# Attention and mixture of experts on one core: full 128-wide tiles for the narrow transposes, and another order in the last batch

## The chip, the core and the metric

The kernel runs on one core of one Trainium2 chip. The metric is device time in microseconds (us). The engines are TensorE (PE in the profile; its weight loads are PEld), VectorE (DVE), ScalarE (ACT), GpSimd (POOL) and SyncE (SP), which here issues most DMAs.

## The reference

For 8 batches (B), 8 heads, 576 tokens (S) and 64 columns a head, keys and values are averaged over 8 neighbouring tokens, so that each head has 72 pooled keys, and attention runs over those. The result, 4608 tokens of 512 columns, goes through a mixture of 4 groups of 4 experts, each expert 512 to 1024 to 512; a token goes to the best expert of its best group.

```python
k_p = k.reshape(B, H, Sp, pool, D).mean(axis=3)          # v_p the same; pool = 8, Sp = 72
scores = scale * np.matmul(q, k_p.transpose(0, 1, 3, 2))
attn = np.exp(scores - scores.max(-1)); attn = attn / (attn.sum(-1) + 1e-09)
x = np.matmul(attn, v_p)                                  # (B*S, H*D), heads side by side
...
g_idx = argmax(x @ w_group); g_w = softmax(x @ w_group)[g_idx]
e_idx = argmax(x @ w_expert[g_idx]); e_w = softmax(...)[e_idx]
out = g_w * e_w * (relu(x @ w1[g, e]) @ w2[g, e])         # float32 in and out
```

## The kernel before

**Tiling.** A batch's 576 queries are cut into five chunks (`CH`), four of 128 and chunk 4 of 64. The four pairs of heads are `g` = 0 to 3; a pair has 144 pooled keys: 128 in a main tile and 16 that are left, the "remainder". All products that must be exact in float32 are made of two parts, a rounded high one and the low rest (`fp32r`): ScalarE copies the high part out of PSUM, VectorE subtracts it to make the low one.

**A chunk's attention** goes through these steps, each a method: `qb` (VectorE transposes the queries, line 283), `sc` (TensorE scores, 289), `mx` and `sb` (VectorE maximum and subtraction, 296 and 302, ScalarE exponential, 303), `su_` (VectorE sum and reciprocal, 308 to 310), `nm` (GpSimd divides: two remainder products at 318, the main one at 322), `px_` (TensorE transposes the remainder's probabilities, 329; ScalarE copies, 330), `pxd` (VectorE low part, 334), `pm` and `pmd` (the same for the main ones: 341, 343, 347). Then `av` (356) multiplies with the values, `rt` (369) makes the router's logits in 40 rows, `route` (377) transposes them to tokens on partitions. Before a batch's chunks, `kb` and `kt` scale and transpose its keys: four full tiles (261) and the remainder's zero-padded ones, `krz` (266).

**The experts.** In each batch one expert, the one that most tokens want, is applied densely to the whole batch: `up` (525; ScalarE relu 527, VectorE low part `upd` 532) in eight blocks of two halves, 256 and 320 tokens, 12 products each; `down` (546, for the 64-token chunk 556; ScalarE scales and writes, 551 and 552) in 14 steps. `split` makes high and low parts of the weights: ScalarE at 510, GpSimd (or VectorE, where the plan says `:v`) at 511. Tokens that wanted another expert (`Left`) are gathered, multiplied and scattered in blocks of 32; here one block holds them, and it runs inside the last batch: `step` (placement), `which` (the block's batch and expert, converted to integers at 661), `fetch_x`, `fetch_a`, `fetch_b` (loads on SP), `whole` and `turn` (add the two parts, transpose, 725 and 735), `gather` (743), `up`, `down` (757, 773; scatter by an indirect DMA on GpSimd).

**Order.** Plans written by hand as strings set the order: START, FIRST (batch 0), STEADY (batches 1 to 6) and LAST (batch 7). In a plan `m.` is the batch whose experts run, `n.` the attention of the next batch, `x.` the one after it, `l.` the leftover. So during batch 3's `up`, TensorE also does the scores and transposes of batch 4. TensorE, SP and VectorE keep the plan's order everywhere; ScalarE and GpSimd do so in START only and are ordered by a scheduler elsewhere. PSUM has three buffers for `mm`, one for `sc`, three for `tp`.

Of the kernel before, what the change touches and what calls it, by code (L numbers as in the profile page):

```python
# [8 lines left out]
F32 = mybir.dt.float32  # L9
# [4 lines left out]
ALU = mybir.AluOpType  # L14
# [71 lines left out]
def attn_moe(ctx: ExitStack, tc: tile.TileContext, q, k, v, wg, we, w1, w2, out):  # L86
# [35 lines left out]

    wr = keep.tile([128, 4, 20], F32, name="wr")
# [24 lines left out]
    krz = wk.tile([32, 2, 2, D], F32, name="krz")  # L148
# [10 lines left out]
    class Att:  # L159


        def __init__(s, b):
            s.b = b
            s.xt = s.lt = s.vp = s.kp = s.rp = s.q = s.rem = None
            s.k, s.v, s.qT, s.p, s.px, s.ss, s.su, s.tp, s.ta, s.m = {}, {}, {}, {}, {}, {}, {}, {}, {}, {}

# [91 lines left out]
        def kt(s):  # L258
# [21 lines left out]
        def qb(s, c):  # L280
            o, n = CH[c]
# [3 lines left out]
        def sc(s, c):  # L285
            n = CH[c][1]
# [5 lines left out]
        def mx(s, c):  # L292
            n = CH[c][1]
# [4 lines left out]
        def sb(s, c):  # L298
            n = CH[c][1]
# [5 lines left out]
        def su_(s, c):  # L305
            n = CH[c][1]
# [5 lines left out]
        def nm(s, c, eng="p"):  # L312
            n = CH[c][1]
            p, su = s.p[c], s.su[c]
            eng = nc.vector if eng == "v" else nc.gpsimd
            px = s.px[c] = sm.tile([128, 2, 3, 2, 16], F32, name="px")
            for z in range(2):
                eng.tensor_tensor(  # L318
                    out=px[0:n, z], op=ALU.mult,
                    in0=p[0:n, z].rearrange("p (y x) s -> p y x s", x=2)[:, :, 1, 56:72].unsqueeze(1).broadcast_to([n, 3, 2, 16]),  # L320
                    in1=su[0:n, z].rearrange("p (y x) -> p y x", x=2)[:, :, 1:2].unsqueeze(1).broadcast_to([n, 3, 2, 16]))
# [547 lines left out]
```

## Time and profile before

| | |
|---|---|
| median of 3 runs | 608.69 us (605.95 to 609.57) |
| profiled execution | 606.4 us, of which the span is 604.6 |
| granted TensorE clock, mean | 0.992 |
| busy: TensorE, VectorE, ScalarE, GpSimd | 587.3 (97%), 391.8 (65%), 279.5 (46%), 258.7 (43%) |
| DMA | 81.31 MB, mean 134 GB/s |

The span runs from the first instruction to the last; the execution's time includes what lies around it. Busy shares are means over the whole span, so they say little of a stage. In rows of the trace a name such as `tp<-ident,px 128*96` is what is written and read, with the shape that is loaded into TensorE; L329 is line 329 of the kernel above. A float32 product, such as a score, counts as two instructions in the trace (a group of four stands as x8), a transpose as one.

### The profile page before, as it was taken

The page shows a single profiled execution, that of the slowest core. Times are in us where ns is not written, and L with a number is a line of the kernel's source. Part 1 is how long each engine was busy: PE and PEld are TensorE (multiplying, and loading weights), DVE is VectorE, ACT ScalarE, POOL GpSimd, SP SyncE. Part 2 cuts the span into 40 slices and gives each one's busy share as a digit, 9 for nine tenths or more (in the row PEclk, how much of TensorE's full clock was granted, in tenths as well). Part 3 has the DMA queues.
Part 4 walks back from the last instruction along what each step waited for, and adds up shares of the span by engine and source line. Part 5 has one row for each costly group of instructions (what it writes and reads, how often), then busy time and mean ns, then how long its engine had stood idle before and what let it go on. Part 6 is the DMA issues. An engine that isn't in the chain of part 4 may idle for free.

```text
span 604.6 us, 10902 instructions
## 1 busy us (share of the span) xinstructions
PE 587.3 (97%) x3863; PEld 527.3 (87%) x3863; DVE 391.8 (65%) x996; ACT 279.5 (46%) x581; POOL 258.7 (43%) x268
## 2 busy tenths in 40 slices
PE   8889999999999999999999999999999999999995
PEld 8888888899978998899978998899978998899874
DVE  4468998599662877459672876459672884347321
ACT  2476554365446445364445445364535543253121
POOL 3366443076416552375406553366225552343100
PEclk9799999999999999999999999999999999999999
DMA  7759135555435460663425561783516200641911
GB/s 195 205 160 212 39 70 131 182 175 125 98 105 191 151 115 37 227 214 53 100 88 195 166 114 35 257 303 83 110 63 220 78 1 2 207 151 52 383 47 41
DMA packets 119209, 81.31 MB, mean 134 GB/s; under 512 B 76774, under 2 KB 95718, under 8 KB 118768
## 3 DMA queue, kind: packets, MB, share of 16 engines
q1 hardware_dynamic: 110464, 70.80, 40.0%
q10 hardware_dynamic: 8656, 9.74, 4.9%
q8 instruction: 32, 0.52, 0.4%
q14 instruction: 25, 0.20, 0.1%
q0 software_dynamic: 32, 0.04, 0.0%
HBM read 75.01 MB, written 28.38 MB: 171 GB/s over the span
## 4 chain that ended last, share of the span: by engine, by line
PE 79%; DVE 10%; DMA 4%; ACT 2%; SPq 2%; issue 1%; POOL 0%; ACTq 0%; POOLq 0%; DVEq 0%
PE mm L525 28%; PE mm L546 26%; PE tp L356 6%; PE sc L289 6%; PE mm L556 5%; DVE kp L208 3%; PE tp L341 2%; SPq L203 2%; DMA wr<-in_moe_w_expert_dram 1%; DVE ht L532 1%; PE tp L329 1%; DMA kv<-in_k_dram 1%; DMA q<-in_q_dram 1%; DMA sw<-in_moe_w_dram 1%; ACT kb L233 1%
## 5 line engine op out<-in xcount | busy, mean ns | idle before, releaser
L525 PE MATMUL mm<-xt,w 128*128 128x256 f32 (+1 forms) x1536 | 222.7, 300 | 1.3 <-DVE ht L532 1.3
L525 PEld LDWEIGHTS mm<-xt,w 128*128 128x128 f32 x1536 | 207.6, 189 | 3.7 <-DVE ht L532 1.5
L546 PE MATMUL mm<-w,ht 128*128 128x512 f32 x768 | 187.8, 396 | 0.0
L546 PEld LDWEIGHTS mm<-w,ht 128*128 128x128 f32 x768 | 140.8, 188 | 29.4 <-issue 0.8
L511 POOL TENSOR_TENSOR w<-sw,w 128x1024 fp32r<-128x1024 f32 x52 | 128.0, 2482 | 81.1 <-ACT w L510 75.6
L527 ACT ACTIVATE ht<-mm 128x256 fp32r<-128x256 f32 (+1 forms) x128 | 52.4, 409 | 112.0 <-PE mm L525 111.2
L532 DVE SCALAR_TENSOR_TENSOR ht<-mm,ht 128x256 fp32r<-128x256 f32 (+1 forms) x192 | 60.4, 345 | 35.6 <-ACT ht L527 35.3
L510 ACT CAST w<-sw 128x1024 fp32r<-128x1024 f32 x64 | 65.7, 1047 | 19.0 <-PE mm L525 9.9
L318 POOL TENSOR_TENSOR px<-p,su 128x96 f32<-128x96 f32 (+1 forms) x80 | 26.7, 355 | 110.6 <-DVE su L310 53.1
L296 DVE TENSOR_REDUCE mx<-sc 128x8 f32<-128x576 f32 (+1 forms) x40 | 30.0, 750 | 37.8 <-PE sc L289 37.8
L289 PE MATMUL sc<-kT,qT 128*128 128x144 f32 (+1 forms) x320 | 48.4, 296 | 1.6 <-DVE dg L387 0.6
L322 POOL TENSOR_TENSOR p<-p,su 128x576 f32<-128x576 f32 (+1 forms) x40 | 46.0, 1149 | 3.1
L289 PEld LDWEIGHTS sc<-kT,qT 128*128 128x128 f32 (+1 forms) x320 | 43.3, 186 | 3.9 <-issue 1.2
L551 ACT ACTIVATE y<-mm,gm 128x512 f32<-128x512 f32 x32 | 21.9, 685 | 34.4 <-PE mm L546 34.3
L361 DVE TENSOR_TENSOR xt<-tp,xt 128x320 fp32r<-128x320 f32 (+2 forms) x68 | 29.5, 439 | 11.5 <-ACT xt L357 9.7
L211 POOL TENSOR_TENSOR kv<-kv 128x512 f32<-128x512 f32 x14 | 18.1, 1292 | 43.8 <-DMA kv<-in_v_dram 35.6
L303 ACT ACTIVATE p<-p 128x576 f32<-128x576 f32 (+1 forms) x40 | 27.3, 683 | 20.2 <-DVE p L302 20.0
L562 DVE TENSOR_TENSOR y<-mm,y 64x512 f32<-64x512 f32 x8 | 5.4, 681 | 44.9 <-ACT y L561 44.9
L308 DVE TENSOR_REDUCE su<-p 128x8 f32<-128x576 f32 (+1 forms) x40 | 29.8, 746 | 5.5 <-ACT p L303 4.5
L357 ACT CAST xt<-tp 128x320 fp32r<-128x320 f32 (+2 forms) x68 | 26.1, 385 | 15.7 <-PE tp L356 13.9
L302 DVE TENSOR_TENSOR p<-sc,mx 128x576 f32<-128x576 f32 (+1 forms) x40 | 30.2, 755 | 3.7
L556 PE MATMUL mm<-w,ht 128*128 128x512 f32 x128 | 30.5, 389 | 0.0
(214 smaller groups left out, 724.5 us busy)
## 6 DMA issues: line engine op xcount, KB each, us to landing
sw<-in_moe_w_dram SPq DMA_DIRECT2D x72, 512.0 KB, 4.1
xscr<-xt SPq DMA_DIRECT2D x8, 2304.0 KB
kv<-in_v_dram SPq DMA_DIRECT2D x16, 512.0 KB
out_dram<-y ACTq DMA_DIRECT2D x32, 256.0 KB, 2.0
q<-in_q_dram SPq DMA_DIRECT2D x112, 72.0 KB, 2.5
kv<-in_k_dram SPq DMA_DIRECT2D x14, 512.0 KB, 5.4
kv<-in_moe_w_dram SPq DMA_DIRECT2D x6, 512.0 KB
ph<-xscr SPq DMA_DIRECT2D x2, 1152.0 KB
```

The costliest lines, as they stand in the source:

```text
L289: nc.tensor.matmul(ps[0:n, g // 2, 144 * (g % 2):144 * (g % 2) + 144], lhsT=s.qT[c][:, g, 0:n], rhs=s.kT[:, g, :], start=(g % 2 == 0), sto ...
L296: red(out=mx[0:n], in_=scv, axis=AX.X, op=ALU.max)
L302: tt(out=p[0:n], in0=scv, in1=mx[0:n].unsqueeze(3).broadcast_to([n, 2, 4, SP]), op=ALU.subtract)
L322: eng.tensor_tensor(out=p[0:n], in0=p[0:n], in1=su[0:n].unsqueeze(3).broadcast_to([n, 2, 4, SP]), op=ALU.mult)
L356: nc.tensor.matmul(ps[:, 0:n], lhsT=flat(l[:, g]), rhs=r, start=(i == 0), stop=(i == len(ops) - 1))
L510: nc.scalar.copy(out=wh, in_=raw)
L511: (nc.vector if eng == "v" else nc.gpsimd).tensor_tensor(out=wl, in0=raw, in1=wh.bitcast(F32), op=ALU.subtract)
L525: nc.tensor.matmul(ps[:, 0:n], lhsT=l[:, kc, fs], rhs=xt[:, r, kc, sl], start=(kc == 0 and i == 0), stop=(kc == 3 and i == 2))
L527: nc.scalar.activation(out=ht[:, sl], in_=ps[:, 0:n], func=AF.Relu)
L532: stt(out=ht[:, at:at + hi - lo], in0=ps[:, lo - o:hi - o], scalar=0.0, in1=ht[:, lo:hi].bitcast(F32), op0=ALU.max, op1=ALU.subtract)
L546: nc.tensor.matmul(ps, lhsT=s.ht[f][:, 640 * l + o:640 * l + o + 128], rhs=s.w[2, f // 2][r][:, f % 2, :], start=(i == 0), stop=(i == 23))
L556: nc.tensor.matmul(ps, lhsT=s.ht[f][:, 512:640], rhs=s.w[2, f // 2][r][:, f % 2, :], start=(i == 0), stop=(i == 15))
```

## The change

From batch 1 on, chunk 4 is rows 448 to 576 (128 wide, `span`), so that its queries, scores, sums and transposes have full tiles; only the last 64 columns are written. Also from batch 1 on, the remainder's probabilities of all four pairs stand in one 128-column tile, made by one GpSimd product and transposed once; ScalarE then makes three copies and VectorE two subtractions, each of 32 partitions. The keys' remainder (`krz`) is padded to 128 rows; the logits are one permanent tile of 128 by 640, zeroed once by GpSimd, and its five transposes are full. In LAST three more splits are on VectorE (`:v`), the leftover's steps stand elsewhere, and the last chunk's `down` is two halves of 256 columns (`half`), the first evacuated and written by ScalarE, the second evacuated by VectorE and written on SP's queue. The two index columns are converted one at a time.

```diff
 LAST = """
-m.up:0:0 m.upd:0:0 m.split:1:2 m.load:2:2 l.step l.step l.step m.up:0:1 m.upd:0:1 l.step l.step l.step m.up:1:0 m.upd:1:0 m.split:1:3 m.load:2:3
...
-m.up:7:0 m.upd:7:0 l.slots m.up:7:1 m.upd:7:1 m.down:0 m.down:1 l.rows m.down:2 m.down:12 m.down:13 m.down:3 l.whole:0 l.whole:1
...
-l.down l.fetch_b m.down:10 m.down:11
+m.split:1:2:p l.step m.split:2:0:v m.load:2:2 m.up:0:0 m.upd:0:0 l.step m.up:0:1 l.step l.step l.step m.up:1:0 m.upd:1:0 l.step l.step
...
+l.fetch_x m.up:5:1 l.tiles m.upd:4:1 m.up:6:0 m.upd:3:1 m.upd:5:0 l.fetch_b:1 m.upd:5:1 m.up:7:0 m.split:2:2:v m.split:2:3:v l.whole:3
+m.up:6:1 l.fetch_a:1 m.up:7:1 m.upd:6:0 m.upd:6:1 l.slots l.whole:4 m.down:0 l.rows m.upd:7:0 m.down:1 m.down:2 m.upd:7:1 l.whole:0
...
+l.next_ l.slots m.down:8 l.hback m.down:13 m.half:3:0   l.down l.fetch_a l.fetch_b l.fetch_x  m.half:3:1
 """
...
+    lt = keep.tile([128, 640], F32, name="lt")
+    nc.gpsimd.memset(lt, 0.0)
...
-    krz = wk.tile([32, 2, 2, D], F32, name="krz")
+    krz = wk.tile([128, 2, 2, D], F32, name="krz")
...
+        def span(s, c):
+
+            return (448, 128, 64) if s.b and c == 4 else (*CH[c], 0)
...
-                nc.tensor.transpose(out=ps[:, 32 * z:32 * z + 32], in_=flat(krz[:, z]), identity=ident[0:32, 0:32])
...
+                nc.tensor.transpose(out=ps[:, 128 * z:128 * z + 128], in_=flat(krz[:, z]), identity=ident)
...
         def sc(s, c):
-            n = CH[c][1]
+            n = s.span(c)[1]
...
+            if s.b:
+
+                px = s.px[c] = px[:, 0:128].rearrange("p (t g s) -> p t g s", t=2, g=NG)
+                eng.tensor_tensor(out=px[0:n], op=ALU.mult,
...
+        def px_(s, c):
+            o, n, w = s.span(c)
+            px = ps_t.tile([128, 512], F32, name="tp")
+            if s.b:
+                s.tp[c, 0] = px
+                nc.tensor.transpose(out=px[:, 0:n], in_=s.px[c][0:n].rearrange("p t g s -> p (t g s)"), identity=ident[0:n, 0:n])
+                nc.scalar.copy(out=s.pr[0:96, 0, o + w:o + n], in_=px[0:96, w:n])
+                for r in (0, 64):
+                    nc.scalar.copy(out=s.pr[r:r + 32, 1, o + w:o + n], in_=px[r + 32:r + 64, w:n])
+            else:
...
+        def pxd(s, c):
...
             for z in range(2):
...
+                tt(out=s.pr[32:64, z, o + w:o + n], in0=s.tp[c, 0][32 * z:32 * z + 32, w:n], in1=s.pr[0:32, z, o + w:o + n].bitcast(F32), op=ALU.subtract)
...
-                nc.tensor.transpose(out=lp[0:n, 40 * c:40 * c + 40], in_=s.lt[0:40, o:o + n], identity=ident[0:40, 0:40])
+                nc.tensor.transpose(out=lp[c // 4][:, 128 * (c % 4):128 * (c % 4) + 128], in_=lt[:, o:o + 128], identity=ident)
...
+        def half(s, c, h):
+
+            o, hs = CH[c][0], slice(256 * h, 256 * h + 256)
+            ps = ps_m.tile([128, 512], F32, name="mm")
+            ops = [(f, l, r) for f in range(8) for l, r in ((0, 0), (0, 1), (1, 0))]
+            for i, (f, l, r) in enumerate(ops):
+                nc.tensor.matmul(ps[:, 0:256], lhsT=s.ht[f][:, 640 * l + o:640 * l + o + 128], rhs=s.w[2, f // 2][r][:, f % 2, hs],
+                                 start=(i == 0), stop=(i == 23))
+            y = sm.tile([128, DM], F32, name="y")
+            if h == 0:
+                nc.scalar.activation(out=y[:, 0:256], in_=ps[:, 0:256], func=AF.Copy, scale=s.a.gm[:, c:c + 1])
+            else:
+                ts(out=y[:, 0:256], in0=ps[:, 0:256], scalar1=s.a.gm[:, c:c + 1], scalar2=None, op0=ALU.mult)
+            (nc.sync if h else nc.scalar).dma_start(out=out[S * s.b + o:S * s.b + o + 128, hs], in_=y[:, 0:256])
...
-            nc.vector.tensor_copy(out=ki[:, 0:2], in_=kk)
+            for x in range(2):
+                nc.vector.tensor_copy(out=ki[:, x:x + 1], in_=kk[:, x:x + 1])
```

TensorE in a middle batch, around chunk 4's scores and transposes (`mm` are up products), before:

```order
L525 MATMUL mm<-xt,w 128x320 x12
L289 MATMUL sc<-kT,qT 64x144 x4
L525 MATMUL mm<-xt,w 128x256 x12
L525 MATMUL mm<-xt,w 128x320 x12
L329 MATMUL tp<-ident,px 96x128 x2
L341 MATMUL tp<-ident,p 128x128 x4
L525 MATMUL mm<-xt,w 128x256 x12
L525 MATMUL mm<-xt,w 128x320 x12
L329 MATMUL tp<-ident,px 96x64 x2
L341 MATMUL tp<-ident,p 128x64 x4
```

and changed:

```order
L552 MATMUL mm<-xt,w 128x320 x12
L297 MATMUL sc<-kT,qT 128x144 x4
L552 MATMUL mm<-xt,w 128x256 x12
L552 MATMUL mm<-xt,w 128x320 x12
L347 MATMUL tp<-ident,px 128x128
L370 MATMUL tp<-ident,p 128x128 x4
L552 MATMUL mm<-xt,w 128x256 x12
L552 MATMUL mm<-xt,w 128x320 x12
L347 MATMUL tp<-ident,px 128x128
L370 MATMUL tp<-ident,p 128x128 x4
```

The 64-wide score group and the pairs of remainder transposes are gone; the order is the same.

VectorE in the last batch, around the index conversion (`ki`), before:

```order
L532 SCALAR_TENSOR_TENSOR ht<-mm,ht 128x256
L511 TENSOR_TENSOR w<-sw,w 128x1024
L532 SCALAR_TENSOR_TENSOR ht<-mm,ht 128x256
L532 SCALAR_TENSOR_TENSOR ht<-mm,ht 128x64
L656 TENSOR_SCALAR kb<-cum,it 128x128
L657 TENSOR_REDUCE kT<-kb 128x1
L658 TENSOR_SCALAR kT<-kT 128x1
L659 TENSOR_SCALAR kT<-kT 128x1
L661 CAST ki<-kT 128x2
L662 TENSOR_SCALAR ki<-ki 128x1
L663 TENSOR_SCALAR ki<-ki 128x1
L532 SCALAR_TENSOR_TENSOR ht<-mm,ht 128x256 x2
```

and changed:

```order
L538 TENSOR_TENSOR w<-sw,w 128x1024
L559 SCALAR_TENSOR_TENSOR ht<-mm,ht 128x256
L688 MEMSET it 128x1
L690 TENSOR_SCALAR kT<-cum 128x1
L691 CAST niti<-kT 128x1
L698 TENSOR_SCALAR kb<-cum,it 128x128
L699 TENSOR_REDUCE kT<-kb 128x1
L700 TENSOR_SCALAR kT<-kT 128x1
L701 TENSOR_SCALAR kT<-kT 128x1
L704 CAST ki<-kT 128x1 x2
L705 TENSOR_SCALAR ki<-ki 128x1
```

The `ht` rows evacuate up products for TensorE. After the weight split the index work now comes behind one of them, not two, takes the counter's reset and another conversion (`niti`) with it, and has two conversions of one column.

TensorE at the end of the last batch (`tp` are the leftover's products and transposes, `mm` the experts' down products), before:

```order
L546 MATMUL mm<-w,ht 128x512 x8
L764 MATMUL tp<-ident,q 128x128 x2
L546 MATMUL mm<-w,ht 128x512 x8
L773 MATMUL tp<-kv,q 32x128 x24
L773 MATMUL tp<-rem,q 32x128 x8
L546 MATMUL mm<-w,ht 128x512 x16
```

and changed:

```order
L807 MATMUL tp<-ident,q 128x128 x2
L598 MATMUL mm<-w,ht 128x512 x8
L568 MATMUL mm<-w,ht 128x256 x24
L816 MATMUL tp<-kv,q 32x128 x24
L816 MATMUL tp<-rem,q 32x128 x8
L568 MATMUL mm<-w,ht 128x256 x24
```

The leftover's last products had 16 down products of 512 columns behind them, and now have a half of 24 products of 256 columns on either side.

## Rows read from the trace of the kernel before

**Rows 1.** Windows: us; PE, PEld, DVE, ACT, POOL busy us; PEclk, DMA share, GB/s.

```profile
262.50:295.40 32.90, 32.90 (x254) 32.20 (x254) 26.33 (x57) 16.07 (x35) 19.08 (x18) 1.00 0.50 129
534.80:562.50 27.70, 26.41 (x197) 26.20 (x197) 20.31 (x66) 10.08 (x21) 10.10 (x5) 1.00 0.35 121
```

**Rows 2.** Timeline of TensorE, batch 3's up half: start, length, instruction.

```profile
267.92 0.38 PE L329 MATMUL tp<-ident,px 128*96 128x128 f32 x2
268.14 0.60 PE L341 MATMUL tp<-ident,p 128*128 128x128 f32 x4
...
271.22 3.45 PE L525 MATMUL mm<-xt,w 128*128 128x256 f32 x24
274.51 0.38 PE L329 MATMUL tp<-ident,px 128*96 128x128 f32 x2
...
280.78 0.38 PE L329 MATMUL tp<-ident,px 128*96 128x128 f32 x2
...
287.70 0.38 PE L329 MATMUL tp<-ident,px 128*96 128x128 f32 x2
...
288.27 3.44 PE L525 MATMUL mm<-xt,w 128*128 128x256 f32 x24
291.64 0.31 PE L329 MATMUL tp<-ident,px 64*96 64x64 f32 x2
...
292.13 1.09 PE L525 MATMUL mm<-xt,w 128*128 128x256 f32 x7
```

**Rows 3.** Timeline of TensorE, batch 3's down half, the keys' transposes.

```profile
318.06 0.60 PE L261 MATMUL tp<-ident,kb 128*128 128x128 f32 x4
...
318.83 3.95 PE L546 MATMUL mm<-w,ht 128*128 128x512 f32 x16
```

**Rows 4.** Groups by shape of VectorE, ScalarE: busy us, mean ns | idle before.

```profile
L283 DVE STREAM_TRANSPOSE qT<-q 128x512 f32<-128x512 f32 x28 | 19.7, 702 | 0.2
L511 DVE TENSOR_TENSOR w<-sw,w 128x1024 fp32r<-128x1024 f32 x12 | 15.9, 1327 | 2.9 <-ACT w L510 2.9
...
L334 DVE TENSOR_TENSOR pr<-tp,pr 32x256 fp32r<-32x256 f32 x32 | 13.3, 417 | 1.0
...
L283 DVE STREAM_TRANSPOSE qT<-q 128x256 f32<-128x256 f32 x7 | 3.0, 435 | 0.0
...
L334 DVE TENSOR_TENSOR pr<-tp,pr 32x128 fp32r<-32x128 f32 x8 | 2.3, 282 | 0.2
...
L330 ACT CAST pr<-tp 96x256 fp32r<-96x256 f32 x32 | 11.6, 361 | 5.1 <-PE tp L329 5.1
```

**Rows 5.** Chain of waits in order of time, first and last batch.

```profile
88.49 0.43 DVE pr L334
...
592.48 1.89 PE tp L773 x64
```

**Rows 6.** Timeline of GpSimd and VectorE, batch 3, chunks 3 and 4.

```profile
289.92 1.14 POOL L322 TENSOR_TENSOR p<-p,su 64x576 f32<-64x576 f32 x1
...
282.17 1.27 DVE L309 TENSOR_SCALAR su<-su 128x8 f32<-128x8 f32 x1
...
288.64 0.16 DVE L309 TENSOR_SCALAR su<-su 64x8 f32<-64x8 f32 x1
```

**Rows 7.** Timeline of GpSimd at the start.

```profile
2.87 0.54 POOL L151 MEMSET vx<- 128x512 f32 x1
```

**Rows 8.** Timeline of the last batch: TensorE, VectorE, ScalarE; idle in brackets.

```profile
554.09 8.42 PE L525 MATMUL mm<-xt,w 128*128 128x320 f32 x60 [1.29 <-DVE ht L532]
...
574.91 1.70 PE L735 MATMUL tp<-ident,ph 128*128 128x128 f32 x12 [0.18 <-DVE ph L725]
...
551.43 2.02 DVE L661 CAST ki<-kT 128x2 int32<-128x2 f32 x1
...
598.26 0.69 ACT L551 ACTIVATE y<-mm,gm 128x512 f32<-128x512 f32 x1 [3.45 <-PE mm L546]
```

**Rows 9.** DMA issues: engine, count, KB each, median us to landing.

```profile
out_dram<-y ACTq DMA_DIRECT2D x8, 128.0 KB, 2.4
```

More of the change, by code (lines that the diff above doesn't have):

```diff
@@ L280, in qb @@
         def qb(s, c):
-            o, n = CH[c]
+            o, n, w = s.span(c)
             s.qT[c] = sm.tile([128, NG, 128], F32, name="qT")
@@ L292, in mx @@
         def mx(s, c):
-            n = CH[c][1]
+            n = s.span(c)[1]
             scv = s.ss[c][0:n, :, 0:288].rearrange("p u (x s) -> p u x s", s=SP)
@@ L298, in sb @@
         def sb(s, c):
-            n = CH[c][1]
+            n = s.span(c)[1]
             scv, mx = s.ss[c][0:n, :, 0:288].rearrange("p u (x s) -> p u x s", s=SP), s.m[c]
@@ L305, in su_ @@
         def su_(s, c):
-            n = CH[c][1]
+            n = s.span(c)[1]
             su = s.su[c] = sm.tile([128, 2, 4], F32, name="su")
@@ L312, in nm @@
         def nm(s, c, eng="p"):
-            n = CH[c][1]
+            n = s.span(c)[1]
             p, su = s.p[c], s.su[c]
             eng = nc.vector if eng == "v" else nc.gpsimd
[L316 to L321, printed above, removed]
+            px = sm.tile([128, 192], F32, name="px")
@@ L330, in px_ @@
-            nc.scalar.copy(out=s.pr[0:96, :, o:o + n], in_=pxv)
-        def pxd(s, c):
-            o, n = CH[c]
-            tt(out=s.pr[32:64, :, o:o + n], in0=s.tp[c, 0][32:64], in1=s.pr[32:64, :, o:o + n].bitcast(F32), op=ALU.subtract)
+            if s.b:
[5 more added lines that the diff above has]
+            else:
+                pxv = s.tp[c, 0] = px[0:96, 0:256].rearrange("p (z t) -> p z t", z=2)[:, :, 0:n]
+                for z in range(2):
+                    nc.tensor.transpose(out=pxv[:, z, :], in_=s.px[c][0:n, z].rearrange("p t g s -> p (t g s)"), identity=ident[0:n, 0:n])
+                nc.scalar.copy(out=s.pr[0:96, :, o:o + n], in_=pxv)
@@ L336, in pm @@
+        def pxd(s, c):
+            o, n, w = s.span(c)
+            if not s.b:
+                tt(out=s.pr[32:64, :, o:o + n], in0=s.tp[c, 0][32:64], in1=s.pr[32:64, :, o:o + n].bitcast(F32), op=ALU.subtract)
+                return
+            for z in range(2):
+                tt(out=s.pr[32:64, z, o + w:o + n], in0=s.tp[c, 0][32 * z:32 * z + 32, w:n], in1=s.pr[0:32, z, o + w:o + n].bitcast(F32), op=ALU.subtract)
         def pm(s, c):
-            o, n = CH[c]
+            o, n, w = s.span(c)
@@ L363, in rt @@
         def rt(s, o, n):
-            if s.lt is None:
-                s.lt = sm.tile([128, S], F32, name="lt", bufs=1)
             sl = slice(o, o + n)
```

45 lines of the change are left out of this document (26 added, 19 removed).

## The prediction

> **What bounds the kernel now.** I read the busy share by stretch first. In the first stretch of [rows 1], the "up" half of a middle batch, TensorE is busy for 32.90 of 32.90 us, VectorE for 26.33, ScalarE for 16.07 and GpSimd for 19.08, at full granted clock. So in the six middle batches (b = 1 to 6, one plan) a microsecond off TensorE is a microsecond off the time as long as VectorE keeps up, and work added to ScalarE or GpSimd costs only by being late. The second stretch, in the last batch, has 26.41 of 27.70: the difference is one wait of 1.29 us, of which below.
>
> The second view is TensorE in order of time [rows 2, 3]. The reader is to take differences of **starts** there: ends are modelled and overlap, but from one group's start to the next is what TensorE gave to it. The third is the groups by shape [rows 4], for the price of what is added; then the chain of waits in the first and last batch [rows 5].
>
> **Middle batches, TensorE.**
> A, the scores of chunk 4, 64 queries to 128. Two pieces of the same make-up, each two remainder transposes, four probability transposes, 12+24 up products and one score group of eight, run 274.51−267.92 = 6.59 us with a full score group and 287.70−280.78 = 6.92 with the 64-wide one [rows 2]. Gain 0.33 a batch.
> B, the remainder's probabilities, two transposes to one. In chunks 0 to 3 the pair takes 268.14−267.92 = 0.22 [rows 2], so one is 0.11 and four chunks save 0.44.
> C, chunk 4's transposes. The pair of 64x96 and the four 64x128 take 292.13−291.64 = 0.49 [rows 2]; full ones take 288.27−287.70 = 0.57, less 0.11 for the second remainder transpose 0.46. The 24 up products ahead of the narrow ones last 291.64−288.27 = 3.37, against 274.51−271.22 = 3.29 ahead of full ones: 0.08 of entry. Gain 0.03+0.08 = 0.11.
> D, the keys: four full transposes and two of 32x32 behind them take 318.83−318.06 = 0.77 [rows 3]; six full ones (two and four) take the 0.57 above. Gain 0.20, in the five middle batches that prepare keys for a later one.
> E, the five logits' transposes, 40 rows to 128. As for D, between 0 and 0.2. They stand right behind ScalarE's copy of the logits, so what TensorE saves there it may wait for; I take 0.06.
> A middle batch saves 0.33+0.44+0.11 = 0.88; six save 5.28, D 5×0.20 = 1.00, E 6×0.06 = 0.36: **−6.64**.
>
> A rule against this: [rows 2] show the piece with narrow score products to be the longer one. The Trainium skill's "TensorEngine Tiling (Array Packing)", in the section Overview, takes dimensions of up to 64 to be the case for smaller tiles, with up to twice the speed; its Key Properties add that a change of mode drains the engine, without a price. By the first alone A, C, D and E would be nothing, by the second what the rows show. The first is rival 2.
>
> **Middle batches, the other engines.** VectorE: two subtractions of 32x128 at 282 ns for one of 32x256 at 417 [rows 4], +0.15 in four chunks; in chunk 4 two for one of 32x128, +0.28; the query transpose of chunk 4 702 ns for 435 [rows 4], +0.27. Together 1.14 a batch against 32.90−26.33 = 6.57 of slack. Chunk 4's reductions and subtractions go from 64 to 128 partitions with the same elements on each; I take nothing, at most what the query transpose adds per column, 0.27 each. ScalarE: three copies of the remainder for one; each is smaller than the one of 361 ns [rows 4], so at most +0.72 a chunk, 3.6 a batch against 16.83 idle. GpSimd has one remainder product for two. The tightest new meeting is chunk 4: its probabilities are ready on GpSimd at 289.92+1.14 = 291.06 [rows 6] and TensorE gets to them just behind 291.64 [rows 2]. TensorE saves 0.33+0.11+0.08 = 0.52 on its way from chunk 4's scores to there, so 0.1 or a little more is left, and VectorE's additions may take that. Zero now, up to 0.2 a batch if late.
>
> **First batch.** VectorE is the chain up to 88.92 [rows 5], so there the added work counts: the query transpose 0.27 and two pairs of subtractions 2×0.15, +0.57. After it TensorE saves one remainder transpose, C and one D, 0.11+0.11+0.20 = 0.42. **+0.15**. The logits' tile is zeroed by one GpSimd memset of 640 columns at the start; one of 512 takes 0.54 [rows 7]. It delays GpSimd's half of the first keys' sum, which is wanted only with VectorE's half, from a later load: hidden; without that cover, +0.7.
>
> **Last batch.** TensorE waits 1.29 us at 554.09 on VectorE, which has just spent 2.02 us on the conversion of two index columns [rows 8]. The change makes it two conversions of one column, which may each be as short as the 0.16 of a small operation [rows 6], and moves the index work, with another short conversion, one evacuation further forward; I take 0.8 of the 1.29, ends 0 and 1.29. Three weight splits move from GpSimd to VectorE at 1327 ns [rows 4], +4.0 in a stretch where VectorE has 27.70−20.31 = 7.4 idle [rows 1]: covered, if spread. Adding up and turning the gathered tokens starts earlier: the 0.18 before 574.91 goes [rows 8] and some of the waiting inside that group, −0.3 (0 to −0.5). Two halves of 24 products of 256 columns replace 24 of 512, the same columns; 0 (to +0.3 if short products cost more per column). The last evacuation has 256 columns, not 512 at 0.69 [rows 8]: −0.3. The last write comes behind the scatter, and that waits for the first half's write, 128 KB. Such a write lands in 2.4 us [rows 9]; with an evacuation of 0.4, two issues and as long a landing for the scatter it is some 5.6 from the first half's end. The leftover's group, 1.89 [rows 5], the second half, 12×256 of its columns' 3.29 for 12×(256+320), so 2.9, and its evacuation, 0.4, are 5.2. So +0.4 (0 to +1). Sum **−1.0**; ends −2.1 and +2.3 (rival 3).
>
> **Sum.** −6.64+0.15−1.0 = −7.5. The profiled execution took 606.4 (span 604.6 and 1.8 around it): 598.9. It is 2.3 below the median of the three runs, 608.69; the mean of it and the three is 607.65, and a new median falls about there, so 607.65−7.5 = **600.1**.
>
> **Rivals.**
> 1. *The gain is partly eaten at chunk 4.* Its fuller work is late on GpSimd or VectorE and TensorE waits 0.5 in each of seven batches: +3.5, 603.6. For it: the 0.1 us that is left there. Against: one GpSimd product fewer ahead of it. 0.12.
> 2. *Narrow tiles are not what costs.* A, C, D and E vanish, as if the extra time belonged to the place: 6×0.44+1.00+0.36 = 4.0, 604.1. That is also the time if the change did not make full tiles of them. For it: one piece against one is little evidence, and C's own groups differ by 0.03. Against: pieces that else are alike, and the same sign at 64 and at 32 rows. The rule named above stands behind it. 0.10.
> 3. *The last batch misfires.* Its three more splits meet on VectorE in front of what TensorE waits for: 4.0 less the 1.7 that the conversion gives up, +2.3 in place of −1.0: 603.4. For it: the changed order has two splits in a row. 0.06.
> 4. *Slower: VectorE becomes the bound.* A small VectorE operation can be held up: [rows 6] show 1.27 us for one that takes 0.16 six us later, +1.1. Ten subtractions of the remainder now stand in the stretch; with seven held VectorE has 26.33+1.14+7.7 = 35.2 against 32.90, +2.3 in six batches, +13.6, less 0.8 elsewhere: 620. It decides from the fifth held, 26.33+1.14+5.5 = 33.0. Against: VectorE's 26.33 holds such delays already for 57 operations, and its sum is what it is. 0.04.
>
> **Numbers.** A measurement of this kernel tells 1% from no change: 602.6 and 614.8 around 608.69. Forecast 0.68, nearly all of it faster (0.63; runs spread by some 3 us); of the first three rivals 0.11 falls under 602.6, the rest within: faster 0.74, same 0.22, slower 0.04. The range goes down to 596: the lowest execution, 605.95, less 6.64, the best last batch, 2.1, and E at its end, 0.84 more, is 596.4. It goes up to 604.5, which takes in rivals 1 to 3.
>
> **What would show it.** TensorE's starts in a middle batch: both kinds of piece at 6.5 (A, B), one remainder transpose at 0.11 (B), 3.29 ahead of chunk 4's transposes (C), 0.57 for the six key transposes (D). The up stretch at 32.0 with TensorE fully busy; a gap ahead of chunk 4's transposes speaks for rival 1, VectorE above 31 for rival 4, a difference left between the pieces for 2. In the last batch, no wait of over 0.5 on the index conversion, and the last evacuation at 0.4. The forecast is wrong if TensorE's busy time falls by 6 us and the span doesn't.

## The result, and the profile after

The changed kernel takes 600.97 us (median of 10 runs, 598.57 to 603.95), the kernel before, run beside it, 606.0 (10 runs, 604.46 to 609.57): a ratio of 0.9915, interval 0.9897 to 0.9932. The forecast of 600.1 is 0.9 away and the range holds the median, but that it came so near is luck: two errors nearly cancel. The base, a mean of four runs, was 607.65 and is now 606.0; and the gain is 5.0 us, not 7.5. With 0.85% the kernel falls just within the 1% that the prediction took for no change, to which I gave 0.22, and not in the case with 0.74.

The profiled execution took 602.18 us (span 600.5), 4.1 us of span less than before. The table cuts the span at the first product of each stage on TensorE, from start to start, in us; for b2 to 4 the value is that of one batch; b1 down and b5 down, left out, are within 0.1 of it. The table also has experiments of the next section: `after_2` and `after_3` are the changed kernel, executed again, narrow4 and oldlast stand for `a_narrow4` and `a_oldlast`.

```
         before b_ki1  after after_2 after_3 narrow4 oldlast keepx_late best2
START     40.50 39.45  40.09  40.70  40.18   39.13   38.87   40.26      39.56
b0 up     48.93 49.07  49.66  49.71  49.58   49.35   49.51   49.58      49.10
b0 down   35.69 35.70  35.61  35.61  35.60   35.61   35.64   35.62      35.41
b1 up     38.74 38.74  38.39  38.38  38.37   38.63   38.42   38.41      38.40
b2-4 up   38.74 38.74  37.87  37.87  37.86   38.24   37.86   37.87      37.89
b2-4 down 29.86 29.86  29.72  29.73  29.71   29.70   29.71   29.74      29.73
b5 up     38.74 38.74  41.05  37.91  39.66   38.25   39.88   37.90      37.87
b6 up     38.78 38.78  37.92  37.93  37.90   38.31   37.94   37.93      37.92
b6 down   27.65 27.64  27.83  27.84  27.81   27.79   27.67   27.83      27.82
last up   27.72 26.17  26.06  26.06  26.06   26.08   27.71   26.06      26.07
last down 42.28 42.14  41.68  41.81  44.84   44.71   41.99   41.96      41.44
```

Down the columns most stages repeat to 0.05 us. START differs by up to 1.8 between executions of the same code there, so no effect of the change can be told from it. Two cells stand out: b5 up (37.9, but 41.05 in `after`) and last down (41.7, but 44.84 in `after_3`). They are the subject of most experiments.

A middle batch went nearly as the steps said. The windows of the kernel after, for the stretches of [rows 1] (us; PE, PEld, DVE, ACT, POOL busy; PEclk, DMA share, GB/s):

```profile
261.25:293.28 32.03, 32.03 (x249) 31.91 (x249) 27.16 (x62) 18.14 (x45) 17.20 (x14) 1.00 0.53 132
532.93:558.97 26.04, 26.04 (x196) 26.04 (x196) 21.03 (x67) 10.98 (x21) 2.90 (x2) 1.00 0.38 130
```

The up stretch is 32.03 for 32.90, with TensorE busy throughout; VectorE has 27.16, where 26.33+1.14 = 27.47 was forecast. The last batch's stretch has lost its wait, and GpSimd nearly all its work. TensorE's timeline in batch 3, to be read against [rows 2]:

```profile
266.67 0.27 PE L347 MATMUL tp<-ident,px 128*128 128x128 f32 x1
266.78 0.60 PE L370 MATMUL tp<-ident,p 128*128 128x128 f32 x4
...
273.15 0.27 PE L347 MATMUL tp<-ident,px 128*128 128x128 f32 x1
...
279.31 0.27 PE L347 MATMUL tp<-ident,px 128*128 128x128 f32 x1
...
281.62 1.14 PE L297 MATMUL sc<-kT,qT 128*128 128x144 f32 x8
282.51 3.44 PE L552 MATMUL mm<-xt,w 128*128 128x256 f32 x24
...
285.79 0.27 PE L347 MATMUL tp<-ident,px 128*128 128x128 f32 x1
286.25 3.43 PE L552 MATMUL mm<-xt,w 128*128 128x256 f32 x24
289.52 0.27 PE L347 MATMUL tp<-ident,px 128*128 128x128 f32 x1
289.63 0.65 PE L370 MATMUL tp<-ident,p 128*128 128x128 f32 x4
290.04 3.14 PE L552 MATMUL mm<-xt,w 128*128 128x256 f32 x22
...
303.76 1.03 PE L404 MATMUL tp<-ident,lt 128*128 128x128 f32 x5
...
316.05 0.60 PE L269 MATMUL tp<-ident,kb 128*128 128x128 f32 x4
316.62 1.63 PE L588 MATMUL mm<-w,ht 128*128 128x512 f32 x6
```

Both kinds of piece now take 6.48 (273.15−266.67 and 285.79−279.31) for 6.59 and 6.92: A and B. One remainder transpose takes 0.11, the 24 products ahead of chunk 4's transposes 3.27 for 3.37 (C; its other part did not come, as the transposes themselves take 290.04−289.52 = 0.52, where they took 0.49), the keys 0.57 for 0.77 (D). What did not come is E: of the five transposes of the logits the first two go ahead, and the third waits, as before, for the end of ScalarE's copy of the logits (0.40 us, started at 303.79).

```profile
303.79 0.40 ACT L397 COPY lt<-tp 40x320 f32<-40x320 f32 x1
```

In the groups by shape (busy us, mean ns | idle before), what answers to [rows 4] is priced as forecast, with VectorE at 702 and 282 ns:

```profile
L291 DVE STREAM_TRANSPOSE qT<-q 128x512 f32<-128x512 f32 x35 | 24.6, 702 | 0.2
L363 DVE TENSOR_TENSOR pr<-tp,pr 32x128 fp32r<-32x128 f32 x56 | 15.8, 282 | 1.6
```

Batch 5 is the same program with the same operations, and lost 3.2 us. Its rows on TensorE, ScalarE, VectorE, GpSimd and SP (start, length, instruction, idle before and what ended it), and the two splits of batch 3:

```profile
401.27 1.69 PE L552 MATMUL mm<-xt,w 128*128 128x256 f32 x12 [0.69 <-DVE y L604]
...
419.18 1.22 PE L297 MATMUL sc<-kT,qT 128*128 128x144 f32 x8 [1.30 <-DVE qT L291]
...
427.99 0.65 PE L370 MATMUL tp<-ident,p 128*128 128x128 f32 x4 [0.55 <-POOL p L340]
...
398.85 1.05 ACT L537 CAST w<-sw 128x1024 fp32r<-128x1024 f32 x1 [3.35 <-PE sc L297]
...
413.63 3.26 DVE L538 TENSOR_TENSOR w<-sw,w 128x1024 fp32r<-128x1024 f32 x1
...
413.40 5.73 POOL L538 TENSOR_TENSOR w<-sw,w 128x1024 fp32r<-128x1024 f32 x2
...
276.09 1.21 DVE L538 TENSOR_TENSOR w<-sw,w 128x1024 fp32r<-128x1024 f32 x1
...
276.73 5.21 POOL L538 TENSOR_TENSOR w<-sw,w 128x1024 fp32r<-128x1024 f32 x2 [1.12 <-ACT w L537]
...
383.41 0.38 SPq L514 DMA_DIRECT2D xscr<-xt  x1
...
385.60 14.17 SPq L530 DMA_DIRECT2D sw<-in_moe_w_dram  x4
```

TensorE waits three times, and by its starts against batch 3 it falls back by 0.9, 1.5 and 0.7 us there. The first wait comes ahead of the split: the late cast holds up ScalarE, and so the evacuation that TensorE needs. Then VectorE's weight split takes 3.26 where it takes 1.21 in batch 3, and the query transpose behind it comes 1.30 late for TensorE. The split began 0.23 after GpSimd's had begun; in batch 3 it began 0.64 ahead. It was late because the weights were: in this batch alone SP first writes 2304 KB to the scratch (for the leftover tokens; elsewhere the same instruction is skipped, in 0.10 us), and the weights are issued behind it. (The row of the cast names TensorE's scores, which end just then; in the trace's signals the last part of the weights landed at 398.77, 0.08 ahead of the cast, as in the other traces below.)

### The profile page after: what moved, and what is told of

Its sections match the earlier page's. It is cut to its first block, busy times and chain, and to the rows that moved or that the text cites. A ratio compares the mean times of both kernels' runs of the same rounds, so it can differ in the third digit from the quotient of the medians.

```text
span 600.5 us, 11021 instructions
## 1 busy us (share of the span) xinstructions
PE 582.1 (97%) x3852; PEld 528.4 (88%) x3852; DVE 400.5 (67%) x1037; ACT 294.3 (49%) x651; POOL 245.2 (41%) x231
## 5 line engine op out<-in xcount | busy, mean ns | idle before, releaser
L588 PE MATMUL mm<-w,ht 128*128 128x512 f32 x744 | 181.1, 395 | 0.0
L588 PEld LDWEIGHTS mm<-w,ht 128*128 128x128 f32 x744 | 136.5, 188 | 27.5 <-issue 0.4
L538 POOL TENSOR_TENSOR w<-sw,w 128x1024 fp32r<-128x1024 f32 x49 | 121.9, 2503 | 74.7 <-ACT w L537 73.4
L554 ACT ACTIVATE ht<-mm 128x320 fp32r<-128x320 f32 (+1 forms) x128 | 52.4, 410 | 84.1 <-PE mm L552 83.2
L329 POOL TENSOR_TENSOR px<-p,su 128x128 f32<-128x128 f32 x35 | 14.3, 409 | 105.7 <-DVE su L318 46.9
L598 PE MATMUL mm<-w,ht 128*128 128x512 f32 x128 | 30.9, 391 | 0.0
L598 PEld LDWEIGHTS mm<-w,ht 128*128 128x128 f32 x128 | 23.9, 188 | 5.1 <-issue 0.2
```

The lines of the kernel that those rows point to most:

```text
L538: (nc.vector if eng == "v" else nc.gpsimd).tensor_tensor(out=wl, in0=raw, in1=wh.bitcast(F32), op=ALU.subtract)
L554: nc.scalar.activation(out=ht[:, sl], in_=ps[:, 0:n], func=AF.Relu)
L588: nc.tensor.matmul(ps, lhsT=s.ht[f][:, 640 * l + o:640 * l + o + 128], rhs=s.w[2, f // 2][r][:, f % 2, :], start=(i == 0), stop=(i == 23))
L598: nc.tensor.matmul(ps, lhsT=s.ht[f][:, 512:640], rhs=s.w[2, f // 2][r][:, f % 2, :], start=(i == 0), stop=(i == 15))
```

## The experiments

The theory: in batch 5 the scratch write makes the weights late, the split on VectorE then begins after GpSimd's and is held until that one's first half ends. (The expectations begin with the two parts as theory T, the late weights, and rival U, the held split.) Rivals: the wide chunk 4 is itself what is late there; or VectorE's long split is a symptom, and the late weights alone are the cause.

**The scratch write cut to a quarter**, the other three quarters left out, in the changed kernel and, as a control, in the kernel before.

```diff
-dma_start(out=xscr[s.b], in_=s.xt.bitcast(F32), cond=left, ...)
+dma_start(out=xscr[s.b][:, :, 0:1], in_=s.xt.bitcast(F32)[:, :, 0:1], cond=left, ...)
-dma_start(out=s.xh[i], in_=xscr[...][:, i], cond=s.some)
+dma_start(out=s.xh[i][:, 0:1], in_=xscr[...][:, i, 0:1], cond=s.some)
```

> The changed kernel with a quarter of the scratch write and read of the leftover's tokens (the other three quarters of those tokens' columns are left out and taken as zero). Theory T: the profile of the changed kernel loses 3.2 us in batch 5's up half (41.05 for 37.87 elsewhere) because the write of 2304 KB goes ahead of the weights on SP's queue (issued 383.41, the weights behind it land at 398.8, 2.6 us after the batch's start), and VectorE and ScalarE, which have more to do now, cannot make that up. Then with 576 KB the weights land before the batch starts, batch 5's up half is 37.9, and the ratio to the kernel before falls from 0.9915 to about 0.987 (3 us of 606 less). Rival U: VectorE's weight split meets GpSimd's by chance (3.26 us for 1.21), whatever the weights do: a wait over 1 us stays in some middle batch and the ratio stays 0.990 to 0.992. Rival V: the 3.2 us are of that one execution: ratio 0.9915.

> The kernel before with a quarter of the same scratch write and read (the rest left out and taken as zero): the control. Theory T: the weights were 0.56 us late there too and it cost nothing (batch 5's up half 38.74 as in all others), so ratio 1.000 (0.998 to 1.001), and less than 0.5 us of it in the last batch, where the read is shorter. If the write costs the kernel before as much, 0.995, and the difference between the kernels is not in it.

In the changed kernel b5 up fell to 37.85, as the theory has it, but the whole came to 607.05, ratio 1.0025 (1.0009 to 1.0040), and in the kernel before to 612.14, 1.0117 (1.0102 to 1.0132). In both, another stage broke: b1 up took 45.47 and 41.65. ScalarE is ordered by a scheduler, and the edit had put a cast of weights that had not landed ahead of batch 1's exponentials:

```profile
133.45 1.05 ACT L537 CAST w<-sw 128x1024 fp32r<-128x1024 f32 x1 [2.62 <-DMA sw<-in_moe_w_dram]
```

So the stage speaks for the theory, and the two times say nothing; as a control of the total it failed. Batch 1 of `a_quarter` shows by accident what batch 5 shows: VectorE's split begins there at 145.25, 0.24 behind GpSimd's at 145.01, and takes 3.25.

**The same write, later**: moved behind the weights' loads in the plan of the middle batches.

```diff
-... n.gates n.keep_x m.down:6 ... w.split:1:1 w.load:2:1 x.sc:0
+... n.gates m.down:6 ... w.split:1:1 w.load:2:1 n.keep_x x.sc:0
```

> The changed kernel with the leftover's scratch write issued behind the two down weights loads of the same half instead of ahead of them. Nothing is left out. Theory T: those weights land in time, batch 5's up half falls from 41.05 to about 37.9 us, ratio 0.987 to 0.988. If the next loads in the queue (the rest of the down weights, the keys of the batch after) are then late for VectorE and TensorE, a new wait of up to 2 us appears later in batch 5 and the ratio is 0.989 to 0.992. Rival U: as the changed kernel, 0.9915.

```profile
386.23 4.10 SPq L530 DMA_DIRECT2D sw<-in_moe_w_dram  x2
...
391.26 0.38 SPq L514 DMA_DIRECT2D xscr<-xt  x1
...
394.64 1.99 ACT L537 CAST w<-sw 128x1024 fp32r<-128x1024 f32 x2
```

b5 up is 37.90, no different from the other batches, with no byte less written. That the chunk's width alone is the cause falls: it is as wide as it was. The whole, 600.88 or 0.9937 (0.9923 to 0.9950), missed what the theory alone expected: another loss, or the spread of START, had to be in the runs; the one trace, of 599.65, does not show it.

**VectorE's split given to GpSimd** in the middle batches.

```diff
-m.up:3:0 m.upd:3:0 m.split:2:1:v n.sc:3
+m.up:3:0 m.upd:3:0 m.split:2:1 n.sc:3
```

> The changed kernel with the one weight split per middle batch that VectorE does given to GpSimd (1.21 us less on VectorE, 2.5 more on GpSimd a batch). Theory T: batch 5 still starts with the late weights (wait of 0.7 to 0.9), but the held split (2.05 of the 3.26 us) is gone; GpSimd's later divisions make TensorE wait at the probabilities' transposes, some 0.3 to 1 us in each of six batches: ratio 0.991 to 0.999. Rival U (the held split is the loss): 0.987 to 0.988.

b5 up is 37.78, and 37.77 to 37.84 in the batches around it, with the write ahead of the weights. That does not settle the second rival: the weights were only 0.48 us late in this execution (the cast's start against the stage's, where it is 0.84 ahead in the batches around), and at 0.50 the changed kernel with VectorE's split loses nothing either (`narrow4`, in the table below). What speaks on that rival is in the trace of `after`: the first 0.9 of the 3.2 us stands ahead of the split, so it is of the late weights alone, and the rest follows a split that is 2.05 longer. The time, 609.34 (1.0074, 1.0056 to 1.0091), is again that of another stage: in b1 up, 47.69, the scheduler had put a sum of the next values on GpSimd, which waited 8.68 us for its load, ahead of the product that TensorE waited for.

```profile
157.66 1.26 POOL L219 TENSOR_TENSOR kv<-kv 128x512 f32<-128x512 f32 x1 [8.68 <-DMA kv<-in_v_dram]
...
159.35 0.47 PE L347 MATMUL tp<-ident,px 128*128 128x128 f32 x1 [4.38 <-POOL px L329]
```

**The changed kernel twice more**, without an edit, to see the loss come and go.

> The changed kernel once more, for a second trace. Theory T (revised): its run-to-run spread (598.6 to 604.0 in ten runs, where the kernel before had 604.7 to 606.4 in thirteen of the last comparison) is batch 5's wait, which comes or not by when the weights land behind the leftover's write, and the start. Then batch 5's up half is anywhere between 37.9 and 41.5 us, batches 2, 3, 4 and 6 are 37.9, and the last batch 26.1 and 41.7 within 0.2. Rival W: the wait is the same in every run (41.0) and the spread lies in the start and the first batch.

> The same as after_2, a third trace: with T batch 5's up half differs from the other two by over 0.3 us in at least one; with W it is 41.0 in all three, and the start and the first batch differ by 1 us or more.

`after_2` (599.93 us) has no loss in batch 5, `after_3` (603.93) half of it, and a new one in the last batch. The cast of the weights and VectorE's split of each, first of `after_2`, then of `after_3`:

```profile
397.18 1.05 ACT L537 CAST w<-sw 128x1024 fp32r<-128x1024 f32 x1 [0.69 <-DMA sw<-in_moe_w_dram]
...
411.97 1.21 DVE L538 TENSOR_TENSOR w<-sw,w 128x1024 fp32r<-128x1024 f32 x1
```

```profile
397.42 1.05 ACT L537 CAST w<-sw 128x1024 fp32r<-128x1024 f32 x1 [1.96 <-DMA sw<-in_moe_w_dram]
...
412.20 3.26 DVE L538 TENSOR_TENSOR w<-sw,w 128x1024 fp32r<-128x1024 f32 x1
```

Both waited for the transfer. Against the start of b5 up, that cast, VectorE's split (its length) and GpSimd's split stand so, with the loss of the stage:

```
             cast    VectorE        GpSimd   loss
before       +0.56   15.24 (1.22)   15.88    0
b_ki1        +0.74   15.44 (1.29)   15.88    0
after_2      +0.30   15.08 (1.21)   15.65    0
narrow4      +0.50   15.29 (1.22)   15.65    0
after_3      +1.21   15.99 (3.26)   15.75    1.8
oldlast      +1.43   16.22 (3.25)   15.98    2.0
after        +2.61   17.39 (3.26)   17.16    3.2
keepx_late   -0.84   15.03 (1.22)   15.67    0
```

In these eight the split is held, by 2.05 us, in the three where it starts after GpSimd's, and in none where it starts ahead. Being late is not enough: at +0.50 and less the changed kernel loses nothing, and the kernel before nothing at +0.74.

**Chunk 4 narrow again**, the rest of the change kept, for terms A and C.

```diff
-return (448, 128, 64) if s.b and c == 4 else (*CH[c], 0)
+return (*CH[c], 0)
```

> The changed kernel with chunk 4 left 64 wide in every batch (terms A and C undone, B, D and E kept). If narrow groups cost what the pieces of the kernel before showed, the up halves of batches 2, 3, 4 and 6 go from 37.87 to 38.31 (0.33+0.11 more), the score group of chunk 4 from 0.88 between starts to 1.12. If the place costs and not the width (rival 2), they stay at 37.9. VectorE has 0.5 us less to do in a batch, so batch 5's wait may be shorter.

b2-4 up is 38.24, 0.38 more than with the wide chunk (forecast 0.44). The piece with the score group takes 285.43−278.62 = 6.81, 0.33 more, which is all of A. Of that, 0.23 is the score group, 1.12 from its start to the next row's, where a full one takes 282.51−281.62 = 0.89 in the changed kernel; most of the rest is in the products ahead of it. C is left with some 0.05 of its 0.11.

```profile
278.62 0.27 PE L347 MATMUL tp<-ident,px 128*128 128x128 f32 x1
...
281.01 1.20 PE L297 MATMUL sc<-kT,qT 128*64 128x144 f32 x8
282.13 3.46 PE L552 MATMUL mm<-xt,w 128*128 128x256 f32 x24
285.43 0.27 PE L347 MATMUL tp<-ident,px 128*128 128x128 f32 x1
```

That settles rival 2: the same piece in the same place, fewer rows, and longer. The whole, 602.84 in its single run, has the loss of 3 us in the last batch that `after_3` has, and tells nothing of A and C.

**The last batch's plan of before, with its two-column conversion**, in the changed kernel (LAST and the conversion as they stood); and the reverse in part, **the kernel before with the one-column conversions alone**:

```diff
-nc.vector.tensor_copy(out=ki[:, 0:2], in_=kk)
+for x in range(2):
+    nc.vector.tensor_copy(out=ki[:, x:x + 1], in_=kk[:, x:x + 1])
```

> The changed kernel with the last batch's plan of the kernel before and one conversion of two index columns. The last batch then takes 27.7+42.3 = 70.0 us as before, against 26.06+41.68 = 67.7: 2.3 us more, of which the wait on the conversion is 1.3 to 1.6. If the gain came from what the earlier batches hand over and not from the order, it stays at 67.7.

> The kernel before with one edit of the change: the two index columns converted one at a time. In the kernel before the conversion of two columns begins at 551.43, while GpSimd's split runs (from 551.03), and lasts 2.02 us, as long as that split has to go; operations of one column beside it take 0.15. Theory H: an operation of one column isn't held up and one of two or more is. Then the two conversions take 0.2 to 0.3 together, TensorE's idle of 1.29 is gone and the last up half falls from 27.7 to 26.2 to 26.4. Rival: whatever stands there is held until GpSimd is done, or the order of the changed plan is what helps: still about 2 us, 27.7.

With the old plan last up is 27.71 and TensorE waits again; with the conversion alone in the kernel before it is 26.17. (The single runs took 601.50 and 603.76 us.) First the row of `a_oldlast`, then those of `b_ki1`:

```profile
549.56 6.66 PE L552 MATMUL mm<-xt,w 128*128 128x320 f32 x48 [1.28 <-DVE ht L559]
```

```profile
550.50 0.22 DVE L662 CAST ki<-kT 128x1 int32<-128x1 f32 x2
...
550.09 4.78 POOL L511 TENSOR_TENSOR w<-sw,w 128x1024 fp32r<-128x1024 f32 x2 [10.88 <-ACT w L510]
```

The two casts of one column take 0.22 together with GpSimd's split running beside them, where the one of two columns took 2.02 [rows 8]. Nearly all of the gain of last up, 1.55 of 1.66, is these two lines; the new plan adds 0.1 there. In last down `a_oldlast` has 41.99 for the 41.68 of `after`, so the plan gives 0.3 at most of the 0.6 gained.

**A version without the meetings**: the late scratch write; the leftover's `whole` all on VectorE, so that GpSimd is idle beside the last batch's index work; batch 1 on the old path (in `span`, `nm`, `px_` and `pxd`). The diff shows the second and the third.

```diff
-(nc.gpsimd if c % 2 else nc.vector).tensor_tensor(
+nc.vector.tensor_tensor(
...
-return (448, 128, 64) if s.b and c == 4 else (*CH[c], 0)
+return (448, 128, 64) if s.b > 1 and c == 4 else (*CH[c], 0)
...
-if s.b:
+if s.b > 1:
...
-if not s.b:
+if s.b <= 1:
```

> The changed kernel with three edits: the leftover's scratch write behind the two down weights loads, all sums of the gathered tokens (whole) on VectorE, batch 1's attention (done in the first batch, where VectorE is the chain) as in the kernel before. Theory T: batch 5's up half is 37.9 in every run; GpSimd no longer runs beside VectorE's five slot operations in the last batch, so those take 1.06 and not 2.07 or 3.10, TensorE doesn't idle nor drop its granted clock there, and the last down half is 41.2 to 41.7 in every run; the first up half goes from 49.6 to 49.0. Ratio 0.985 to 0.988 against 0.9915, and a spread of runs below 3 us. If the three waits have others right behind them: 0.990 to 0.992.

> The same without the third edit (batch 1's attention as in the changed kernel): first up half 49.6 and ratio 0.001 above that of the other, 0.986 to 0.989, by theory T; equal to it if the first batch's VectorE chain does not set its time.

`best` took 604.31 (0.9983, 0.9971 to 0.9996), `best_b`, without the third edit, 605.52 (1.0000, 0.9984 to 1.0015): neither is the gain expected. Moving `whole` to VectorE put its fourth piece, in VectorE's fixed order, ahead of the last up blocks' evacuation, and it waits for the scratch to be read:

```profile
556.36 0.69 DVE L768 TENSOR_TENSOR ph<-ph,pl 128x512 f32<-128x512 f32 x1 [4.45 <-DMA pl<-xscr]
...
557.44 3.15 PE L552 MATMUL mm<-xt,w 128*128 128x320 f32 x12 [4.22 <-DVE ht L559]
```

On GpSimd that wait had cost nothing. The third edit did what it should: b0 up 48.93 for 49.62.

```diff
-... m.split:2:2:v m.split:2:3:v l.whole:3
+... m.split:2:2:v m.split:2:3:v
-l.whole:1 l.whole:2 l.turn:1
+l.whole:1 l.whole:2 l.whole:3 l.turn:1
```

> The three edits of the run best, with the sum of chunk 3's gathered tokens placed on VectorE behind the other sums and not two splits ahead of TensorE's last up products, where it waited 4.2 us for the scratch read and held up what TensorE needs. Theory T: last up half 26.1 again and last down half 41.2 to 41.6 without GpSimd beside VectorE's slot operations (1.06 for the five), first up half 48.9, batch 5 37.9: span 596 to 597 with a start of 40, ratio 0.985 to 0.988, spread below 3 us. If the sums on VectorE now make TensorE wait at the gathered tokens' transposes: a wait there of 0.5 to 1.5 and 0.988 to 0.990.

With that step behind the others, `best2` takes **598.25 us** (597.59 to 598.68 in four runs), ratio 0.9870 (0.9853 to 0.9887): 8.2 less than before, 2.7 less than the change by the medians, and the two intervals do not meet. The spread is 1.1 us, in four runs, where the changed kernel spreads over 5.4 in ten. In all four traces with the late write (`keepx_late`, `best`, `best_b`, `best2`) b5 up is 37.83 to 37.90. What each of the edits gives was not taken apart, but for the 0.6 to 0.7 of the third in b0 up. Its index work:

```profile
555.49 1.06 DVE L731 TENSOR_SCALAR q<-kp,kT 128x128 f32<-128x128 f32 x5
...
556.30 1.26 PE L737 MATMUL tp<-kT,q 128*128 128x2 f32 x10
```

## Why the prediction was right, and where not

**A, B and D held, C about half, E did not.** Up is 0.87 shorter a batch (A, B, C: 0.88 forecast), down 0.14 (D and E: 0.26). D came to its 0.20, and a product behind it, which counts the tokens (L437), waits 0.08 longer than before. E failed at what I named as its risk: the transposes wait for ScalarE.

**FIRST was +0.65, not +0.15.** VectorE's additions cost 0.73 in b0 up (0.57 forecast). The 0.42 that was to come back later did not; b0 down is 0.08 shorter.

**LAST was about −2.0, not −1.0.** Last up gave 1.66, where I took 0.8 of a wait of 1.29: the wait itself and what followed from it are gone. Last down gave 0.6 in `after`, with an end that is shorter by the evacuation (0.48 for 0.69) and two halves that cost 0.2 more. b6 down is 0.18 longer, by a split that LAST now takes first (27.67 with the old plan). The second half's length, 2.9, is in the working what 24 products of 256 columns give, not the 12 that it names; the first half took 589.82−586.85 = 2.97. The last write, for which the working has +0.4, was issued at 595.65, 0.23 behind the end of its evacuation.

**The step that failed is the cover: "Together 1.14 a batch against 32.90−26.33 = 6.57 of slack"**, and with it rival 4's question of how many operations are held in a whole stretch. The slack is there. In batch 5 VectorE is busy 31.26 us of 41.05 and in batch 3, over the same stage, 31.11 of 37.87: its sum is the same, and 3.2 us are lost. What decides is the moment of one instruction. From the starts in the table, GpSimd's (15.65 after the change, 15.88 before) and VectorE's (14.78 and 14.69 plus the cast's lateness), I estimate that the split is held when the weights come 0.87 us late after the change, and 1.19 before. The stage also starts 10.64 us behind the weights' issue, not 10.92: some 0.6 us of margin gone in all, in transfers that vary by 2 us (they landed 11.0 to 13.2 behind their issue). Of the 0.6 only 0.09 is VectorE's later start; 0.23 is GpSimd's earlier one and 0.28 the earlier stage, so most of it is not VectorE's added work. That the kernel before would lose as much at the same lateness was not tried; its runs spread by 1.8 us in twenty, but by 5.1 in the ten beside the changed kernel. I had read one execution, in which the weights came 0.56 late and so short of the 1.19, and asked of no transfer how near it was.

The Trainium skill's "SBUF — State Buffer", in the section "Who interferes with whom", gives the rule that fits: VectorE and GpSimd share a pair of ports, and for certain VectorE operations whoever issues first holds it for the whole instruction, while the other is blocked. The trace agrees, in the eight rows of starts above and in the 2.05 us, for 2.17 to 2.18 that GpSimd's first piece still had to go. By the Trainium skill's "VectorE: DVE Perf Modes", section "What auto-detection actually checks", an operation with one source, both sides in SBUF, takes both ports where the outermost dimension of more than one element is even, or equal, in source and destination. That fits the conversion of two columns, which was held for 2.02 us; a single column has no such dimension, the section does not speak of it, and here it was not held (0.22 for two). I had the case before me, 1.27 for 0.16 in [rows 6], and priced it as a matter of how many operations, not of when.

**The last batch's loss in some executions** is the same meeting: five operations of VectorE on the index tiles, beside GpSimd's `whole`, which starts when the scratch has been read. They take 1.06 alone (`best2`), 2.07 in `after`, 3.10 in `after_3`. The rows of `after`, then of `after_3`:

```profile
559.84 2.07 DVE L731 TENSOR_SCALAR q<-kp,kT 128x128 f32<-128x128 f32 x5
...
560.44 2.62 POOL L768 TENSOR_TENSOR ph<-ph,pl 128x512 f32<-128x512 f32 x2 [23.58 <-DMA pl<-xscr]
```

```profile
558.42 3.10 DVE L731 TENSOR_SCALAR q<-kp,kT 128x128 f32<-128x128 f32 x5
...
558.83 2.60 POOL L768 TENSOR_TENSOR ph<-ph,pl 128x512 f32<-128x512 f32 x2 [23.39 <-DMA pl<-xscr]
...
561.57 0.38 PE L737 MATMUL tp<-kT,q 64*128 64x2 f32 x2 [0.83 <-DVE q L731]
561.88 5.54 PE L588 MATMUL mm<-w,ht 128*128 128x512 f32 x16
```

and its windows (columns as above):

```profile
559.00:561.00 2.00, 1.35 (x10) 1.12 (x8) 2.00 (x3) 0.00 (x0) 2.00 (x2) 1.00 1.06 409
561.00:563.00 2.00, 1.43 (x6) 1.23 (x7) 1.86 (x8) 0.00 (x0) 0.43 (x1) 0.87 1.05 390
563.00:565.00 2.00, 2.00 (x7) 1.51 (x6) 1.27 (x3) 0.00 (x0) 0.00 (x0) 0.50 1.08 354
```

Held twice, TensorE has 1.35 and 1.43 busy of 2.00 in two windows, some of it on products of two columns, and then the granted clock is 0.50, the lower of its two levels (1.2 of 2.4 GHz): 16 down products take 5.38 us for 3.77. Waits of 1.2 us (0.39 and 0.83) become 3.0 of time. `narrow4` shows the same (44.71, clock 0.50). In `after`, held once, the clock stays at 1.00.

**Rival 1** came in one batch of seven, and with 0.38 for its 0.5. In b1 TensorE, faster now, stands before chunk 4's probabilities. VectorE's split is held there (2.35 at 126.52), but it was as long before (2.58 at 126.29) and cost nothing; that the wait comes of it is not shown. Rival 3's wait did not come: TensorE is busy throughout last up, 26.04 of 26.04.

```profile
154.44 0.66 PE L370 MATMUL tp<-ident,p 128*128 128x128 f32 x4 [0.38 <-POOL p L340]
```

**The sum.** Where batch 5 loses nothing (`after_2`) the span is 6.44 shorter: START +0.20, batch 0 +0.70, batches 1 to 6 −5.4, LAST −1.95. Against the forecast, −6.64, +0.15 and −1.0, the middle batches miss 1.2: b1 0.5, E 0.06 and the counts' product 0.08 in each of six or five. The other 1.4 us to the 5.0 of the medians I put down to the meetings, which come in some executions and not in others: three of the five traces of the changed program with the write ahead and VectorE's split (`narrow4` and `oldlast` among them) lost 1.8 to 3.2 in batch 5. Run by run this is not shown, as the runs without a trace tell no stage. What sets the length of START was not settled.

## What to carry to other kernels

Slack of an engine over a stretch is no cover for an addition: ask which of its instructions starts just ahead of another engine's that can hold it, and what the latest transfer in any batch does to that order. Judge a step by its stage in the trace, and look at every stage: an edit that a scheduler sees can move work far away, and three of these experiments had their time decided in batch 1 by an edit that was meant for batch 5. Where executions of one kernel differ by several us, compare the traces of two of them stage by stage: the stage that differs has lost a margin, and that may be worth more than the next instruction.

## What the runs showed of the hardware that was not expected

- A held VectorE operation waits until GpSimd's piece ends, however small it is itself: 2.02 us for a conversion of 128x2, 1.27 on 128x8 [rows 6], for the 0.17 that the same operation takes at 274.75, 3.26 for 1.21 on 128x1024. Casts of 128x1 were not held at all beside the same split (0.22 for two).
- Narrower is slower between full tiles: a score group with 64 rows takes 1.12 us and with 128 rows 0.89, start to start.
- Behind a write of 2304 KB on the same queue the load of the weights landed 11.0 to 13.2 us after its issue, differently in each execution (loads of this size take 4.4 in the median of `after`). The lateness is that of one part: of the sixteen signals that tell its landing, fifteen had come 0.19 us ahead of the stage in `after`, and the last came 2.53 behind its start; in `after_3` 0.49 ahead and 1.13 behind.
- Two waits of TensorE, of 0.39 and 0.83 us, with products of two columns between them, were followed by a granted clock of 0.50, and the stage took 3.0 us more; behind a single one of 0.36 the clock stayed at 1.00 (`after`).
